# Loads in a line of four, halved first steps, and attention in 64x32 tiles of TensorE, in a fused attention and feed-forward kernel

## The chip, the cores and the metric

The kernel runs on one core of a Trainium2 chip. The metric is the device time of one execution in microseconds (us). A profile of one execution gives, for each engine, when every instruction ran and what it waited for: TensorE (PE, with its weight loads as PEld), VectorE (DVE), ScalarE (ACT), GpSimd (POOL), and SyncE (SP), whose queue issues the DMAs.

## The reference

A linear attention with a quadratic feature map, and a feed-forward block on its result. There are 4 batches, 4 heads, 1088 positions, 32 dimensions per head, r = 8; the block has 4352 tokens of 128 and 2048 hidden units.

```python
def phi(x):
    a = np.einsum('rd,bhsd->bhsr', S1, x)
    b = np.einsum('rd,bhsd->bhsr', S2, x)
    return np.einsum('bhsi,bhsj->bhsij', a, b).reshape(*x.shape[:-1], r * r)
q_p, k_p = (phi(q), phi(k))
kv = np.einsum('bhsf,bhsd->bhfd', k_p, v)
z = np.sum(k_p, axis=2)
num = np.einsum('bhsf,bhfd->bhsd', q_p, kv)
den = np.einsum('bhsf,bhf->bhs', q_p, z)[..., None] + 1e-06
x = num / den                       # heads side by side: 4352 x 128
h = x @ w_in
out = (h * np.clip(h + 3.0, 0.0, 6.0) / 6.0) @ w_out
```

## The kernel before, in words

Tokens lie along the free dimension, in nine chunks: eight of 512 and one of 256 that gathers the ends of all four batches. Each chunk goes through eight steps in the feed-forward block; a step makes 256 hidden units.

*Keys, per batch* (`keys`, `features`): kT is loaded in two groups of 4 and 5 tiles of 128 positions. PE projects them (`abps_k`), ACT copies the result (`ab_k`), POOL or DVE forms the 64 products per head (`ph_k`), PE sums products times v over all positions (`kvps`, 33 columns: 32 of v and one of ones), and ACT copies the sums to `kvb`, in which two heads' blocks stand diagonally.

*Queries of chunks 0 and 1* (`queries`): the same projection and products, then PE transposes the products (`phps`), ACT copies them (`phT`), PE forms numerators and denominators (`nd`, in `divided`), DVE divides (`norm`), PE transposes x (`xt`, into `xps`), and `split` makes of x a rounded part `xh` on ACT and the rest `xl` on DVE or POOL.

*Queries of chunks 2 to 8, called far* (`far_queries`): the projection is two matmuls with 64 weight columns (`mm_far`, tile `abps_q`, L457), DVE transposes in blocks of 32 (`cp_far`, `turn`), and the full transposition goes through DRAM: `wr` writes four pieces (`phd`, L667), `rd` reads them back as `phT` (L672). `nd` then runs in two halves of 256 tokens, each matmul with 32 tokens as weights, all 128 rows and 66 columns (two heads), so that half of the products are with zeros.

*Feed-forward step* (`step`): w_in and w_out come as 64-bit words and are split into a high and a low part by nine DVE and ACT operations per block of 512 (`convert_steps`, tiles `cva_wi`, `cva_wo`). A step takes h = wi_hi xh + wi_lo xh + wi_hi xl (L723, L724, L729), ACT's relu, DVE's gate (`g`), ACT's rounded part (`gh`), POOL's or DVE's rest (`gl`), and three products per 128 units into the output bank `o` (L768, L769, L771).

*Order.* Everything is entered into a list (`Plan`) with a cost per engine, a due time and the buffers it holds. `Plan.order` plays the list through in time and so fixes the order on every engine; the hardware then runs each engine's list in that order. The due times come from constants (`STEP`, `DUES`, `LAG`, `LEADS`, `W_DUE`, `CONV_LEAD`, `LOAD_DUE`). Until 17 us of planned time PE gets filler matmuls (`warm`, L326) where it would be idle. PSUM is three pools: h (2 of two banks), o (2), a (2). In fp32, the profile counts two matmul instructions and two weight loads for each matmul call of the attention. All loads go on SP's queue as soon as the plan has them due and a buffer is free; nothing else holds them back.

Of the kernel before, what the change touches and what calls it, by code (L numbers as in the profile page):

```python
# [15 lines left out]
F32 = mybir.dt.float32  # L16
F32R = mybir.dt.float32r
# [5 lines left out]
P = 128  # L23
HP = P // 2
# [26 lines left out]


# [8 lines left out]
START = {PE: 0.6, ACT: 4.2, DVE: 4.05, POOL: 2.0, SP: 1.18}  # L61
# [3 lines left out]
S_READY = 4.6  # L65
# [9 lines left out]


# [7 lines left out]
STEP = 4.6  # L84
DUES = (154.74, -15.16, 342.66, 122.47)
LAG = 20.51
W_DUE = (-264.43, 162.57, -10.3, 9.86, 223.59, -14.56, -8.54, 128.42)
CONV_LEAD = (-233.02, -43.68, 143.73, 134.72, 228.69, 90.47, 237.81, 136.67, 12.66)
LOAD_DUE = {'kT_0': -98.0, 'wiraw0': -99.0, 'kT_1': -97.0, 'kT_3': -89.0, 'qT_1': -96.0, 'v_3': -95.0, 'v_0': -94.0, 'qT_0': -90.0, 'v_1': -93.0, 'woraw0': -87.0, 'v_2': -88.0, 'kT_2': -92.0, 'wiraw1': -91.0}
LEADS = ({'ab': -122.75, 'cp': -223.0, 'ph': 236.37, 'kv': 270.92, 'kvb': 259.6, 'tr': -22.42, 'trcp': -414.87, 'nd': -219.64, 'norm': 20.99, 'xt': 200.47, 'xh': -420.54, 'xl': 165.56, 'k0': -152.92, 'kld': 94.09, 'vld': 12.64, 'qld': -163.5, 'rd': -4.41, 'xw': 26.17, 'xr': -69.62}, {'ab': 51.61, 'cp': 372.76, 'ph': -99.12, 'kv': 10.45, 'kvb': -57.07, 'tr': -243.35, 'trcp': -85.14, 'nd': 171.45, 'norm': -61.11, 'xt': 74.34, 'xh': 39.91, 'xl': 385.1, 'k0': 34.47, 'kld': 59.11, 'vld': 69.81, 'qld': 111.37, 'rd': 68.22, 'xw': 337.32, 'xr': -5.08}, {'ab': -408.45, 'cp': -279.52, 'ph': 530.56, 'kv': -494.27, 'kvb': 166.7, 'tr': -30.0, 'trcp': -36.58, 'nd': 2.26, 'norm': 255.85, 'xt': -99.65, 'xh': 32.03, 'xl': -230.05, 'k0': 396.51, 'kld': 294.01, 'vld': 22.2, 'qld': 35.72, 'rd': 273.5, 'xw': -349.65, 'xr': 50.89})  # L90


HOLD = 21.82
HOLD_DUE = -27.43
SOON = 22.85
SOON_DUE = 316.94
PATIENCE = 0.75
# [34 lines left out]
class Plan:  # L132
# [56 lines left out]

    def order(self):  # L190
# [9 lines left out]
        while left:  # L200
# [13 lines left out]
            for op in avail:  # L214
                if op.ready > t and len(op.cost) == 1 and all(b.held or any(free[g] for g in b.tags) for b in op.bufs):
                    soon[next(iter(op.cost))].append((op.ready, op.due))
            began = []
            for op in avail:
                if op.ready > t or not all(b.held or any(free[g] for g in b.tags) for b in op.bufs):
                    continue  # L220
# [77 lines left out]
def fused_kernel(ctx: ExitStack, tc: tile.TileContext, qT, kT, v1, sb, w_in, w_out, outT):  # L298
# [73 lines left out]

    def load(tag, shape, name, src, due, dtype=F32, view=None):
        b = Buf((tag,))
        box = []

        def emit(_):
            t = buf(tag, shape, name, dtype)
            box.append(t)
# [5 lines left out]
        return plan.add({SP: ISSUE}, LOAD_DUE.get(name, due), (), emit, [b], moved=n * mybir.dt.size(dtype) / 1e3), b, box  # L385

# [15 lines left out]
    nc.vector.tensor_tensor(s_sb, s_sb, low, op=ALU.add)  # L402
    s_ab = const.tile([P, 2, H, R], F32, name="s_ab")
    nc.scalar.copy(s_ab, s_sb.rearrange("p (h s r) -> p s h r", s=2, r=R))
# [8 lines left out]

    def weights(j, due_i, due_o):
        c = slice(j * WB, (j + 1) * WB)
        for nm, src, view, hi, lo, due, acc in (
            ("wi", w_in[:, c], None, wi_hi, wi_lo, due_i, wi_ops),
            ("wo", w_out_v[:, j * 4 : (j + 1) * 4, :], lambda t: t.rearrange("p (f d) -> p f d", d=P), wo_hi, wo_lo, due_o, wo_ops),
        ):
# [170 lines left out]
    def split(c, due, T, last, xpb, xhb, LEAD):  # L590
# [15 lines left out]
        if xpb.tags == ("xT",):  # L606
            cost = {POOL: 2.35 * n / 1024, **cost}
# [249 lines left out]
```

## Time and profile before

| | |
|---|---|
| three runs | 245.06, 245.56, 245.86 us (median 245.56) |
| the profiled execution | 245.6 us, of which the span from first to last instruction is 243.4 us |
| mean granted TensorE clock | 0.985 |
| busy share of the span: PE, PEld, DVE, ACT, POOL | 97, 75, 75, 67, 58% |
| DMA | 23.82 MB in 18008 packets, mean 98 GB/s |
| first hidden-layer matmul | 24.09 us after the span's start |

A page of the profile gives busy time per engine, the span in 40 slices (a digit is the busy share in tenths; PEclk is the granted clock in tenths of full speed), the DMA queues, the chain of work that ended last, and the costliest groups of instructions. "L557" is a line of the kernel; a count such as x64 is of instructions. Matmuls overlap, so a group's mean duration is longer than the distance from one to the next; the chain's pieces give the latter.

### The profile page before, as it was taken

Reading aid. Unit: us, or ns where it says so; the run is one execution under the profiler, and the core shown is the slowest. Engines: PE = TensorE matmul, PEld = TensorE weight load, DVE = VectorE, ACT = ScalarE, POOL = GpSimd, SP = SyncE. Lnnn points to the kernel's source line nnn. Section 1 sums busy time; section 2 is a strip of 40 time slices with the busy share of each in tenths; the row PEclk is TensorE's granted clock in tenths of the full one; section 3 lists DMA queues with packets and bytes.
Section 4 is the critical chain, followed back from the end, with each engine's and each line's share of the span. In section 5 each row is a group of like instructions: output and inputs, shape, how many; then the busy total and the mean of one; then the engine's idle time right before and its main releaser. Section 6 shows DMA issues by size and latency. Waiting matters only on the chain.

```text
span 243.4 us, 5531 instructions
## 1 busy us (share of the span) xinstructions
PE 234.9 (97%) x2281; PEld 182.4 (75%) x2281; DVE 183.0 (75%) x251; ACT 163.3 (67%) x204; POOL 141.7 (58%) x87
## 2 busy tenths in 40 slices
PE   8949999999999999999999999999999999999994
PEld 2737767676777778877788888888888787888894
DVE  3928999999999689899698875666566676466662
ACT  4425669648859756577399877667777666767771
POOL 2514969976799999249055745444433534944340
PEclk9967999999999999999999999999999999999999
DMA  6996752432033624884443100001000111010010
GB/s 210 383 402 237 256 176 58 151 90 86 3 90 103 168 80 130 212 268 125 137 91 77 46 12 31 0 4 43 0 0 3 43 43 43 3 43 0 0 46 22
DMA packets 18008, 23.82 MB, mean 98 GB/s; under 512 B 1728, under 2 KB 11072, under 8 KB 17984
## 3 DMA queue, kind: packets, MB, share of 16 engines
q1 hardware_dynamic: 17984, 23.48, 30.6%
q8 instruction: 18, 0.29, 0.5%
q14 instruction: 6, 0.05, 0.1%
HBM read 16.26 MB, written 7.21 MB: 96 GB/s over the span
## 4 chain that ended last, share of the span: by engine, by line
PE 91%; issue 2%; DMA 2%; ACT 2%; DVE 1%; SPq 0%
PE h L723 14%; PE h L729 13%; PE o L771 13%; PE o L768 13%; PE h L724 13%; PE o L769 13%; PE nd L557 4%; PE kvps L514 3%; DMA kT<-kT_dram 2%; PE abps_k L452 2%; PE abps_q L457 2%; PE phps L629 1%; PE warm L326 1%; ACT g L736 1%; PE abps_q L452 1%
## 5 line engine op out<-in xcount | busy, mean ns | idle before, releaser
L747 POOL TENSOR_TENSOR gl<-g,gh 128x1024 fp32r<-128x1024 f32 (+1 forms) x45 | 106.4, 2373 | 65.1 <-ACT gh L743 60.4
L739 DVE SCALAR_TENSOR_TENSOR g<-g,h 128x1024 f32<-128x1024 f32 (+1 forms) x72 | 83.0, 1157 | 37.2 <-ACT g L736 36.9
L736 ACT ACTIVATE g<-h 128x1024 f32<-128x1024 f32 (+1 forms) x72 | 70.1, 977 | 35.9 <-PE h L729 35.2
L743 ACT CAST gh<-g 128x1024 fp32r<-128x1024 f32 (+1 forms) x72 | 71.8, 1000 | 14.9 <-DVE g L739 11.8
L723 PE MATMUL h<-xh,wi_hi 128*128 128x512 f32 (+1 forms) x144 | 56.4, 392 | 0.2 <-DVE g L739 0.2
L729 PE MATMUL h<-xl,wi_hi 128*128 128x512 f32 (+1 forms) x144 | 55.4, 386 | 0.0
L724 PE MATMUL h<-xh,wi_lo 128*128 128x512 f32 (+1 forms) x144 | 55.0, 382 | 0.0
L768 PE MATMUL o<-gh,wo_hi 128*128 128x512 f32 (+1 forms) x144 | 55.0, 384 | 0.0
L769 PE MATMUL o<-gh,wo_lo 128*128 128x512 f32 (+1 forms) x144 | 54.5, 381 | 0.0
L771 PE MATMUL o<-gl,wo_hi 128*128 128x512 f32 (+1 forms) x144 | 43.8, 386 | 0.0
L747 DVE TENSOR_TENSOR gl<-g,gh 128x1024 fp32r<-128x1024 f32 (+1 forms) x27 | 31.5, 1171 | 1.7 <-ACT gh L743 1.5
L723 PEld LDWEIGHTS h<-xh,wi_hi 128*128 128x128 f32 x144 | 27.0, 187 | 6.8 <-DVE g L739 0.7
L768 PEld LDWEIGHTS o<-gh,wo_hi 128*128 128x128 f32 x144 | 27.0, 188 | 6.3 <-ACT kvb L539 0.4
L729 PEld LDWEIGHTS h<-xl,wi_hi 128*128 128x128 f32 x144 | 27.0, 187 | 6.0
L769 PEld LDWEIGHTS o<-gh,wo_lo 128*128 128x128 f32 x144 | 27.0, 187 | 5.6
L724 PEld LDWEIGHTS h<-xh,wi_lo 128*128 128x128 f32 x144 | 27.1, 188 | 5.4
L771 PEld LDWEIGHTS o<-gl,wo_hi 128*128 128x128 f32 x144 | 25.9, 187 | 6.2 <-POOL gl L747 0.8
L480 POOL TENSOR_TENSOR ph_k<-ab_k 128x512 f32<-128x512 f32 (+1 forms) x15 | 14.9, 1009 | 15.5 <-ACT ab_k L461 15.5
L480 POOL TENSOR_TENSOR ph_q<-ab_q 128x512 f32<-128x512 f32 x13 | 13.7, 1069 | 3.5 <-DVE ab_q L465 3.5
L557 PEld LDWEIGHTS nd<-kvb,phT 128*32 128x32 f32 (+1 forms) x480 | 9.3, 119 | 3.6 <-issue 3.1
L602 POOL TENSOR_TENSOR xl<-xT,xh 128x512 fp32r<-128x512 f32 x4 | 6.2, 1550 | 9.0 <-ACT xh L598 9.0
L557 PE MATMUL nd<-kvb,phT 128*32 128x66 f32 (+1 forms) x480 | 11.2, 229 | 0.0
(70 smaller groups left out, 165.3 us busy)
## 6 DMA issues: line engine op xcount, KB each, us to landing
phd<-pht SPq DMA_DIRECT2D x24, 128.0 KB, 2.2
phT<-phd SPq DMA_DIRECT2D x6, 512.0 KB, 4.4
wiraw<-w_in_dram SPq DMA_DIRECT2D x4, 512.0 KB, 5.4
qT<-qT_dram SPq DMA_DIRECT2D x8, 256.0 KB, 4.7
woraw<-w_out_dram SPq DMA_DIRECT2D x4, 512.0 KB, 5.9
outT_dram<-os SPq DMA_DIRECT2D x8, 256.0 KB, 2.0
xd<-xt SPq DMA_DIRECT2D x24, 64.0 KB, 1.8
xT<-xd SPq DMA_DIRECT2D x6, 256.0 KB, 2.7
```

The lines of the kernel that those rows point to most:

```text
L480: engines[e].tensor_tensor(out, a_, b_, op=ALU.mult)
L557: nc.tensor.matmul(W["nd"][e : e + w, o : o + 2 * DV], T["phT"][:, p, i : i + w], kvb[batch_of(c0 + i)][:, p, :], start=True, stop=True)
L723: nc.tensor.matmul(T["h"][:, u, :n], wi_hi[:, f], x, start=True, stop=False)
L724: nc.tensor.matmul(T["h"][:, u, :n], wi_lo[:, f], x, start=False, stop=False)
L729: nc.tensor.matmul(T["h"][:, u, :n], wi_hi[:, f], x, start=False, stop=True)
L736: nc.scalar.activation(T["g"][:, :, :n], T["h"][:, :, :n], AF.Relu, bias=3.0, scale=1.0)
L739: nc.vector.scalar_tensor_tensor(T["g"][:, :, :n], T["g"][:, :, :n], 6.0, T["h"][:, :, :n], op0=ALU.min, op1=ALU.mult)
L743: nc.scalar.copy(T["gh"][:, :, :n], T["g"][:, :, :n])
L747: engines[e].tensor_tensor(T["gl"][:, :, :n], T["g"][:, :, :n], T["gh"][:, :, :n].bitcast(F32), op=ALU.subtract)
L768: nc.tensor.matmul(o, wo_hi[:, f], T["gh"][:, u, :n], start=first and u == 0, stop=False)
L769: nc.tensor.matmul(o, wo_lo[:, f], T["gh"][:, u, :n], start=False, stop=False)
L771: nc.tensor.matmul(o, wo_hi[:, f], T["gl"][:, u, :n], start=False, stop=last and u == 1)
```

## The change

1. *Loads.* `FIRST_LOADS` fixes the order of the first 13 loads. From the fifth on, load k has a gate: a POOL copy of one column from the tile of load k - 4 into the tile of load k, which makes it wait for that load's landing and makes load k wait for the copy. All other loads come after the last gate.
2. *Projection weights.* DVE writes `s_ab` (needed first) and ACT copies it to `s_sb`; before, the other way round.
3. *Halves.* For chunk 0 `split` makes `xh` and `xl` in two halves of 256 tokens, each after its own transposition, and its first two steps run their matmuls on each half.
4. *Far projection.* Eight matmuls of 64 rows by 32 weight columns by a quarter of the chunk, for two, into two PSUM banks (one per pair of heads in the upper or lower 64 rows); `cp_far` is two transposes.
5. *Far quotients.* `divided_far` replaces the two halves of `nd`: 64 matmuls of 64 rows by 32 weight columns by 33 columns per 512 tokens, for 32 of 128 rows by 66 columns; the upper 64 rows write one bank, the lower another. `norm` is one operation over both banks.
6. *Write to DRAM.* `wr` issues eight writes per far chunk, for four, half as long each.
7. *Plan.* `room` counts buffers for operations that take two of one pool; all due times and the rules for choosing between engines have new values.

The diff, cut to its core:

```diff
+HALVED = 1
+FIRST = 2
...
-START = {PE: 0.6, ACT: 4.2, DVE: 4.05, POOL: 2.0, SP: 1.18}
+START = {PE: 0.6, ACT: 4.45, DVE: 4.05, POOL: 2.0, SP: 1.18}
...
-S_READY = 4.6
+S_READY = 4.2
...
+AHEAD = 4
+FIRST_LOADS = ("kT_0", "wiraw0", "kT_1", "qT_0", "v_0", "v_1", "qT_1", "woraw0", "kT_2", "wiraw1", "v_2", "woraw1", "qT_2")
...
-STEP = 4.6
-DUES = (154.74, -15.16, 342.66, 122.47)
-LAG = 20.51
+STEP = 6.02
+DUES = (153.97, 226.88, 170.52, 441.39)
+LAG = 31.93
...
+        rank = FIRST_LOADS.index(name) if name in FIRST_LOADS else 0
+        ahead = loads[FIRST_LOADS[rank - AHEAD]] if rank >= AHEAD else None
...
+        def gate(_):
+            old = ahead[2][0].bitcast(U32) if ahead[3] != F32 else ahead[2][0]
+            new = tile().bitcast(F32) if dtype != F32 else tile()
+            nc.gpsimd.tensor_copy(first(new), first(old))
...
+        deps = gates[-1:] if name not in FIRST_LOADS else []
+        if ahead:
+            deps = [plan.add({POOL: 0.12}, due, [ahead[0]], gate, [ahead[1], b])]
+            gates.extend(deps)
...
         def mm_far(_):
-            T["ps"] = bank(pb.tag, f"abps_{name}")
-            for e in (0, HP):
-                nc.tensor.matmul(T["ps"][e : e + HP, : n * HP], s_sb, src[0][:, e * n : (e + HP) * n], start=True, stop=True)
+            T["pss"] = [bank(b.tag, f"abps_{name}_{p}") for p, b in enumerate(pbs)]
+            w = n * Q
+            for p, g in product(range(2), range(4)):
+                r = slice(p * HP, (p + 1) * HP)
+                nc.tensor.matmul(
+                    T["pss"][p][g * Q : (g + 1) * Q, :w],
+                    s_sb[r, p * Q : (p + 1) * Q],
+                    src[0][r, g * w : (g + 1) * w],
+                    start=True,
+                    stop=True,
+                    tile_position=(p * HP, g * Q),
+                )
...
+        def nd(_):
+            W["nd"] = [bank(b.tag, f"nd_{c}_{r}") for r, b in enumerate(nbs)]
+            for t, p, g, r in product(range(nt), range(2), range(4), range(2)):
+                o = (2 * t + p) * DV
+                i = t * P + g * Q
+                f = slice(r * F, (r + 1) * F)
+                nc.tensor.matmul(
+                    W["nd"][r][g * Q : (g + 1) * Q, o : o + DV],
+                    T["phT"][f, p, i : i + Q],
+                    kvb[batch_of(c0 + i)][f, p, r * DV : (r + 1) * DV],
+                    start=True,
+                    stop=True,
+                    tile_position=(r * F, g * Q),
+                )
...
+            for r in range(2):
+                nc.vector.tensor_scalar(den[:, r], nds[r][:, :, D : D + 1], 1e-6, None, op0=ALU.add)
+            nc.vector.reciprocal(rden, den)
...
+            for r in range(2):
+                nc.vector.tensor_tensor(x[:, r], nds[r][:, :, 0:D], rden[:, r].broadcast_to([P, k, D]), op=ALU.mult)
...
+        ranges = [(0, n // 2), (n // 2, n)] if c < HALVED else [(0, n)]
...
-            for e, p in product(range(2), range(2)):
-                k = (2 * e + p) * Q
-                nc.sync.dma_start(d[p, :, :, e * n // 2 : (e + 1) * n // 2].rearrange("f r x -> r f x"), T["turn"][k : k + Q])
+            w = n // 4
+            for g in range(4):
+                src = T["turn"][g * Q : (g + 1) * Q].rearrange("r f (p x) -> r f p x", p=2)
+                for p in range(2):
+                    nc.sync.dma_start(d[p, :, :, g * w : (g + 1) * w].rearrange("f r x -> r f x"), src[:, :, p])
...
+        halved = c < HALVED and fp < FIRST
+        for r, u in product(range(2 if halved else 1), range(2)):
```

More of the change, by code (lines that the diff above doesn't have):

```diff
@@ L100 @@
+HOLD = 9.88
+HOLD_DUE = -2.07
+SOON = 28.52
+SOON_DUE = 75.42
+PATIENCE = 0.61
 @dataclass(eq=False)
@@ L188, in choose, with room @@
         return idle[0]
+    @staticmethod
+    def room(op, free):
+        taken = []
+        for b in op.bufs:
+            if not b.held:
+                g = next((g for g in b.tags if free[g] > taken.count(g)), None)
+                if g is None:
+                    return False
+                taken.append(g)
+        return True
     def order(self):
@@ L214, in order @@
             for op in avail:
-                if op.ready > t and len(op.cost) == 1 and all(b.held or any(free[g] for g in b.tags) for b in op.bufs):
+                if op.ready > t and len(op.cost) == 1 and self.room(op, free):
                     soon[next(iter(op.cost))].append((op.ready, op.due))
@@ L218, in order @@
             for op in avail:
-                if op.ready > t or not all(b.held or any(free[g] for g in b.tags) for b in op.bufs):
+                if op.ready > t or not self.room(op, free):
                     continue
@@ L552, in nd @@
             W["nd"] = bank(nb.tag, f"nd_{c}_{t}")
-            w = HP if c < NEAR else Q
-            for u, p, e in product(range(m), range(2), range(0, P, w)):
+            for u, p, e in product(range(m), range(2), (0, HP)):
                 o = (2 * u + p) * 2 * DV
                 i = (t + u) * P + e
-                nc.tensor.matmul(W["nd"][e : e + w, o : o + 2 * DV], T["phT"][:, p, i : i + w], kvb[batch_of(c0 + i)][:, p, :], start=True, stop=True)
+                nc.tensor.matmul(W["nd"][e : e + HP, o : o + 2 * DV], T["phT"][:, p, i : i + HP], kvb[batch_of(c0 + i)][:, p, :], start=True, stop=True)
         def norm(_):
@@ L674, in far_queries @@
         a = plan.add({DVE: 0.09 + 0.27 * nt}, due - LEAD["tr"], sorted(set(o3), key=o3.index), turn, [phb, turnb])
-        a = plan.add({SP: 4 * ISSUE}, due - LEAD["trcp"], [a], wr, [turnb], moved=n * 1.024)
+        a = plan.add({SP: 8 * ISSUE}, due - LEAD["trcp"], [a], wr, [turnb], moved=n * 1.024)
         rdop = plan.add({SP: ISSUE}, due - LEAD["rd"], [a], rd, [phTb], moved=n * 1.024)
-        norms = []
-        for t in range(0, nt, 2):
-            norms.append(divided(c, due, T, t, min(2, nt - t), rdop, phTb, Buf(ndb), xb, LEAD))
+        norms = [divided_far(c, due, T, rdop, phTb, [Buf(ndb), Buf(ndb)], xb, LEAD)]
         if mixed:
```

154 lines of the change are left out of this document (100 added, 54 removed).

## The prediction

> **What bounds the kernel now.** I read the page first (shares, slices, chain), then the busy table by stage, the chain over the first 24 us, the DMA counts there, and last the chain's far pieces.
>
> ```profile
> span 243.4 us, 5531 instructions
> PE 234.9 (97%) x2281; PEld 182.4 (75%) x2281; DVE 183.0 (75%) x251; ACT 163.3 (67%) x204; POOL 141.7 (58%) x87
> PEclk9967999999999999999999999999999999999999
> PE 91%; issue 2%; DMA 2%; ACT 2%; DVE 1%; SPq 0%
> ```
> TensorE is the bound: 97% busy and 91% of the chain. Only the third and fourth slice show a lower clock. The same by stage (columns: length, then busy and count of PE, PEld, DVE, ACT, POOL; clock; DMA share; GB/s):
> ```profile
> 0.00:12.16 12.16, 10.89 (x222) 6.11 (x222) 7.62 (x18) 5.20 (x12) 4.42 (x13) 1.00 0.84 296
> 12.16:15.57 3.41, 0.00 (x1) 0.00 (x0) 0.48 (x1) 0.08 (x1) 0.00 (x0) 0.80 1.07 390
> 15.57:21.06 5.49, 5.49 (x85) 4.45 (x86) 2.98 (x9) 2.39 (x5) 2.09 (x2) 0.50 0.99 377
> 24.09:240.20 216.11, 215.48 (x1921) 169.82 (x1919) 169.19 (x221) 153.25 (x183) 134.25 (x72) 1.00 0.25 75
> ```
> From the first hidden-layer matmul (24.09) to the last output matmul, PE idles 0.63 of 216.11 us. So time can come only from the first 24 us, or from PE work that gets shorter. The start holds both a dead stretch of 3.41 us, with every engine idle and only DMA at work, and 5.49 us at clock 0.50. The chain there:
> ```profile
> 12.16 3.41 issue
> ...
> 16.05 1.01 PE abps_k L452 x32
> 17.06 1.96 PE nd L557 x32
> ...
> 19.87 0.54 PE warm L326
> ...
> 20.84 0.61 PE warm L326 x2
> ...
> 21.67 0.21 PE warm L326
> ```
> The same work at full clock, and a far projection (columns: start, length, what, count of instructions):
> ```profile
> 28.61 1.24 PE nd L557 x32
> ...
> 53.13 0.58 PE abps_k L452 x32
> 57.64 0.58 PE abps_q L457 x4
> ```
> "Issue" means that PE waited for nothing that the profile shows. I take it for code that hasn't arrived, and argue it from the DMA counts: the whole run's, those of the stall, and what was issued and moved up to 8.3 us.
> ```profile
> q8 instruction: 18, 0.29, 0.5%
> ```
> ```profile
> q1 hardware_dynamic: 1010, 1.31, 104.9%
> q8 instruction: 1, 0.02, 1.7%
> ```
> ```profile
> q1 hardware_dynamic: 1024, 2.11, 74.8%
> issues: line engine op xcount, KB each, median us to landing
> wiraw<-w_in_dram SPq DMA_DIRECT2D x2, 512.0 KB, 5.4
> qT<-qT_dram SPq DMA_DIRECT2D x3, 256.0 KB, 6.9
> v<-v_dram SPq DMA_DIRECT2D x2, 330.0 KB, 5.6
> kT<-kT_dram SPq DMA_DIRECT2D x2, 256.0 KB, 5.1
> woraw<-w_out_dram SPq DMA_DIRECT2D x1, 512.0 KB, 7.4
> kT<-kT_dram SPq DMA_DIRECT2D x1, 320.0 KB, 4.6
> v<-v_dram SPq DMA_DIRECT2D x1, 264.0 KB, 5.6
> sb_raw<-sb_dram SPq DMA_DIRECT2D x1, 64.0 KB, 1.8
> ```
> 18 packets for PE's 4,562 matmuls and weight loads make some 253 instructions a packet. PE stopped after 222 + 222 = 444 of them, a little short of two packets, and the run's first packet moved inside the stall (the counts of 0 to 12.16 us hold none). It would be asked for when one packet was used up, near 8 to 9 us. By 8.3 us the issued loads sum to 4,124 KB (4.22 MB) and 2.11 MB had moved, so 2.11 MB stood in line: 5.4 us at 390 GB/s, which sets a late-comer's turn at 13.7 us, inside the stall. So the packet queued behind the loads.
>
> **The change, part by part.** Sums go against the profiled execution: 243.4 span, 245.6 in all, so 2.2 us lie around the span; the median of the runs is 245.56.
>
> *Loads in line of four.* The first 13 loads keep at most four in flight: a one-column POOL copy waits for the load four places ahead and frees the next. Four neighbours hold at most 512 + 256 + 512 + 264 = 1,544 KB (1.58 MB, 4.0 us of line). The gate and the issue come after the landing, so often only three are moving (about 1.03 MB, 2.6 us). Against 5.4 us the packet comes 1.4 to 2.8 us sooner, and the stall falls from 3.41 to between 0.6 and 2.0; I take 1.4, a gain of 2.0. With a short stall the clock should hold for the most part. At 0.50 nd took 1.96 and abps_k 1.01, at full clock 1.24 and 0.58: 1.15 lost there, some 0.25 more in the projection beside them; I take 1.0 of the 1.4 back. The gates stand on POOL ahead of the key products, behind loads that land by 5 to 8 us; if one lands late, POOL's product and then kv wait for it, and the loads behind wait in SP: bounded by the gain itself, since line and stall are the same bytes. The projection weights made one DVE step earlier save an ACT copy that waits for kT_0 anyway: nothing.
>
> *Halved first steps.* Chunk 0's two norms come one after the other; splitting x lets the first hidden matmul follow the first. It can only replace the filler ("warm" 0.54 + 0.61 + 0.21 = 1.36); I take 0.8. The columns streamed are the same. The start in all: 2.0 + 1.0 + 0.8 = 3.8 (bounds 0 and 3.41 + 1.4 + 1.36 = 6.2).
>
> *Far quotients and projections in 64x32 tiles.* Far nd, the matmul after it, and kv, whose shape is near:
> ```profile
> 60.97 1.06 PE nd L557 x64
> 62.03 0.43 PE h L729
> ...
> 68.95 0.70 PE kvps L514 x60
> ...
> 88.23 0.60 PE nd L557 x32
> ```
> Far nd stands in the chain four times as x64 and five as x32: 4 x 1.06 + 5 x 0.60 = 7.24 us. After, each of six and a half chunks has 64 matmuls of two instructions, 128 for 64, with 33 columns for 66 on eight tiles for four. No row here has two row bands at work. If the bands overlap wholly, an instruction costs a quarter of 1.06/64 = 16.6 ns, 4.1 ns, 0.53 a chunk; if not at all, it costs what kv's 33-column one does, 0.70/60 = 11.7 ns, 1.50 a chunk. Both ends are equally near in shape (kv has the columns, nd the operands), so I take the middle, 1.0: 6.5 us, 0.7 less (bounds: 3.8 less, 2.5 more). One nd for two saves two re-entries; the matmul after one takes 0.43 for 0.23: 0.4.
> Weighed against this, the Trainium skill's "TensorEngine Tiling (Array Packing)", section Instruction Overhead, says that a matmul costs some 60 cycles however few its columns, and not to tile a dimension that is already small. By it 33 columns cost nearly what 66 do, nd would be 128 x 8.3 ns = 1.06 a chunk, and the sum would lose the 0.7; kv's 11.7 ns at half of nd's columns leans that way.
> The projection: 0.58 for 4 instructions of 256 columns on two tiles becomes 16 of 128 columns on eight. Fully overlapped 0.29, without the bands 0.58; nearer the overlap, since halved weights already run side by side in kv and nd: 0.40, six and a half times 0.18 = 1.2 less (bounds 1.9 and 0). PE work in all: 0.7 + 0.4 + 1.2 = 2.3 less.
>
> *Around the tiles.* Two banks are now held at once by projection and by quotient, of the two that "a" has; the x64 pieces already used both. On DVE two transposes stand for one, and one reciprocal goes:
> ```profile
> L465 DVE STREAM_TRANSPOSE ab_q<-abps_q x7: 318/450/451, 22.6 to 191.4; 128x256 f32<-128x256 f32 x6, 128x128 f32<-128x128 f32 x1
> L566 DVE RECIPROCAL rden<-den 128x8 f32<-128x8 f32 x17 | 3.5, 203 | 0.6
> ```
> 2 x 0.318 - 0.450 = +0.19, less 0.20: nothing. If DVE were late, the next far chunk's projection would wait for both banks; DVE is busy 169 of the 216 us. SP issues eight writes for four per far chunk:
> ```profile
> 50.45 1.80 SPq L667 DMA_DIRECT2D phd<-pht  x4
> ```
> ```profile
> 54.45 0.38 SPq L672 DMA_DIRECT2D phT<-phd  x1
> ```
> ```profile
> phT<-phd SPq DMA_DIRECT2D x6, 512.0 KB, 4.4
> ```
> That is 1.8 us more before phT is read back, and later loads queue behind it. Chunk 2's read lands at 54.45 + 4.4 = 58.9, its nd starts at 60.97: the cover is 2.1 us, so 1.8 is hidden, barely. Without cover, PE would stand up to 1.8 for the first far chunk; later ones can be started earlier. *The new due times* reorder all engines; from 24.09 on PE has 0.63 us to win and everything to lose, so I count nothing.
>
> Sum: 3.8 + 2.3 = 6.1 off the span: 237.3, and 239.5 in all.
>
> **Rivals.**
> *A. The code doesn't come sooner.* The line is shorter, but the stall and the cold clock stay. For it: DMA is saturated (share 1.07) with four in flight too, and the link from line to stall is inferred. Against: line and delay agree (13.7 against a packet inside the stall). Then only the 2.3 and 0.5 of the halves come: 240.6 span, 242.8. The Trainium skill's "DMA: Bandwidth & Descriptors", section Queues, rings and completion order, says that each DMA engine takes turns between queues after every packet; by that rule a code packet wouldn't wait for the whole line, which would be this rival, and the trace's agreement with a full line speaks against it.
>
> *B. The row bands don't run together.* Nothing in the trace shows that they do. Then nd is 2.5 dearer, the projection unchanged: 243.4 - 3.8 + 2.5 - 0.4 = 241.7 span, 243.9.
>
> *C. Slower: code runs out in the quotients.* A far nd is now 128 matmuls and 128 weight loads, 256 instructions: a whole packet in about 1 us, where half of one went before. If each of the seven bursts ends in a wait for the next packet (in the stall's counts 1.7% of 16 engines over 3.41 us, 0.93 us of transfer alone), PE idles seven times. It decides from (6.1 + 0.7)/7 = 1.0 us a burst; at 1.3 the span is 243.4 - 6.1 + 9.1 = 246.4, 248.6 in all. For it: the stall at 12.16 is this very thing. Against:
> ```profile
> 25.00:30.00 5.00, 5.00 (x217) 3.73 (x216) 4.72 (x10) 2.75 (x6) 5.00 (x7) 1.00 0.74 255
> ```
> 433 instructions went through in 5 us with PE never idle and DMA at 0.74; and a burst stands between hidden-layer steps, which use only 45 instructions in 5 us, so the next packet has time.
>
> **How the numbers follow.** My forecast (start and tiles both pay, 236 to 242) has 0.60, A 0.14, B 0.14, C 0.12. The time is that of the forecast, 239.5. Its own range goes from 236.0 (start 6.2, tiles 3.4) to 242.0 (start 1.9, tiles 1.7). The range takes in A and B and leaves out C and the extremes: 235.8 to 244.6. About 0.3% (0.74 us) is what a measurement of this kernel can tell from no change. Faster by more (below 244.8): the forecast, A and B but for the cases where a poor start and unpaired bands meet, 0.81. Within it: 0.07. Slower: C, 0.12.
>
> **What would show it.** The chain's issue piece after 12 us: about 1.4 or shorter, and the first code packet before 13 us. The granted clock: at most one stretch at 0.50 before 25 us. The first hidden matmul by 20.3 us (24.09 - 3.8) or sooner. Far nd: one x128 piece near 1.0 us a chunk; the far projection, x16, near 0.40. From there to the end PE idle under 1.5 us. The prediction is wrong if the stall is still over 3 us (A), if nd takes 1.4 (B), if issue pieces of 1 us follow the nd pieces (C), or if PE now waits in the first 60 us for DVE's weight conversions or, in nd, for phT: none of these is in the sum.

## The result: slower by 3%, and the profile after

The changed kernel took 253.40 us (median of 4 runs, 251.84 to 255.22) beside 245.47 for the kernel before: a ratio of 1.033 (1.026 to 1.039). Run again later with the experiments it gave 252.01 (6 runs), ratio 1.025 (1.021 to 1.029). The forecast was 239.5, with 235.8 to 244.6. Ratios here compare undisturbed executions only, so one can lie a little off the quotient of the two medians; a point is one per cent of the kernel before. The profiled execution took 252.8, with a span of 251.0 against 243.4.

The page of the changed kernel (span, busy row, granted clock, PE's code queue, shares of the chain):
```profile
span 251.0 us, 6639 instructions
PE 235.6 (94%) x2788; PEld 184.7 (74%) x2788; DVE 191.5 (76%) x261; ACT 162.6 (65%) x205; POOL 129.1 (51%) x90
PEclk9999779999999999999999999999999999999999
q8 instruction: 22, 0.36, 0.6%
PE 81%; DMA 8%; DVE 4%; issue 3%; SPq 2%; ACT 0%; DVEq 0%
```
PE's busy time rose by 0.7 us (234.9 to 235.6), and its idle time from 8.5 to 15.4 us: nine tenths of the loss is waiting. PE has 2 x 507 instructions more and needs 22 code packets for 18. Where it waits, by stage (columns as in the table before):
```profile
0.00:12.13 12.13, 10.56 (x221) 6.04 (x222) 6.73 (x16) 5.11 (x11) 6.13 (x21) 1.00 0.75 246
...
13.65:33.04 19.39, 13.24 (x434) 10.18 (x433) 15.52 (x34) 6.92 (x16) 7.53 (x8) 0.91 0.92 322
33.04:60.00 26.96, 25.92 (x301) 19.83 (x298) 22.62 (x33) 20.98 (x29) 24.04 (x18) 0.94 0.18 55
60.00:125.00 65.00, 62.83 (x1067) 48.16 (x1066) 52.49 (x80) 41.21 (x47) 55.93 (x28) 1.00 0.44 128
```
The first hidden-layer matmul starts at 33.04 instead of 24.09. Up to it PE idles 9.24 us (33.04 less the 10.56 and 13.24 busy), where it was 4.69 of 24.09; from 33 to 60 it idles 1.04, and from 60 to 125 another 2.17. The chain in the start, and then, from the timeline (start, length, engine, line, operation, tiles), the last pieces of chunk 0's x, which the first hidden step needs:
```profile
12.13 1.52 issue
...
24.55 1.71 issue
...
27.52 1.42 PE kvps L595 x80
28.94 0.94 PE abps_k L521 x34
29.88 2.42 issue
...
33.10 0.51 PE h L850
```
```profile
19.00 0.37 ACT L720 CAST xh<-xps 128x256 fp32r<-128x256 f32 x1
19.40 0.76 DVE L724 TENSOR_TENSOR xl<-xps,xh 128x256 fp32r<-128x256 f32 x2
```
Chunk 0's x is whole at 20.16 (19.40 + 0.76), and DVE finishes the low part of the first block of w_in at 14.48. Yet the hidden layer waits 13 us more, because in the new order PE must first issue key projections (abps_k), key-value sums (kvps) and transposes of other chunks. These are short instructions in great number. Up to the first hidden matmul PE stops three times for "issue", 5.65 us in all, two of them (4.13) after x is whole; in the start before it stopped once, for 3.41. Beside these stand waits for data. PE's table of waits (in all, how often, the longest):
```profile
PE abps_k L521 <- issue: 4.1, 2, 2.4
PE h L850 <- DVE g L867: 1.9, 2, 1.0
PE abps_k L521 <- DMA kT<-kT_dram: 1.5, 2, 0.9
PE abps_q L521 <- issue: 1.5, 1, 1.5
PE nd L666 <- issue: 1.3, 1, 1.3
PE abps_k L521 <- DVE x L648: 1.0, 1, 1.0
```
Issue comes to 6.9 us, where the whole run before had 3.4 + 0.4; data waits (for DVE and for keys) to 4.4, where it had 0.6 (for DVE and ACT). So there are two candidates of about the same size, code and data.

### The profile page after: what moved, and what is told of

It is laid out like the page before. It is cut to its first block, busy times and chain, and to the rows that moved or that the text cites. A ratio compares the mean times of both kernels' runs of the same rounds, so it can differ in the third digit from the quotient of the medians.

```text
span 251.0 us, 6639 instructions
## 1 busy us (share of the span) xinstructions
PE 235.6 (94%) x2788; PEld 184.7 (74%) x2788; DVE 191.5 (76%) x261; ACT 162.6 (65%) x205; POOL 129.1 (51%) x90
## 4 chain that ended last, share of the span: by engine, by line
PE 81%; DMA 8%; DVE 4%; issue 3%; SPq 2%; ACT 0%; DVEq 0%
PE h L850 13%; PE o L896 12%; PE o L899 12%; PE o L897 12%; PE h L856 12%; PE h L851 12%; DMA kT<-kT_dram 5%; PE nd L666 3%; PE kvps L595 3%; PE abps_k L521 2%; DMA xT<-xd 2%; DMA phT<-phd 2%; DVE xl L724 1%; SPq L817 1%; DVE g L867 1%
## 5 line engine op out<-in xcount | busy, mean ns | idle before, releaser
L875 POOL TENSOR_TENSOR gl<-g,gh 128x1024 fp32r<-128x1024 f32 x38 | 91.7, 2427 | 82.9 <-ACT gh L871 62.5
L875 DVE TENSOR_TENSOR gl<-g,gh 128x1024 fp32r<-128x1024 f32 (+1 forms) x34 | 37.7, 1110 | 1.0 <-ACT gh L871 1.0
L850 PEld LDWEIGHTS h<-xh,wi_hi 128*128 128x128 f32 x148 | 28.3, 191 | 9.8 <-DVE g L867 3.5
L856 PEld LDWEIGHTS h<-xl,wi_hi 128*128 128x128 f32 x148 | 28.3, 191 | 5.8 <-issue 0.2
L851 PEld LDWEIGHTS h<-xh,wi_lo 128*128 128x128 f32 x148 | 28.4, 192 | 5.2
L561 POOL TENSOR_TENSOR ph_k<-ab_k 128x512 f32<-128x512 f32 (+1 forms) x17 | 16.5, 992 | 14.5 <-ACT ab_k L540 10.8
L561 POOL TENSOR_TENSOR ph_q<-ab_q 128x512 f32<-128x512 f32 x14 | 16.2, 1174 | 1.7 <-DVE ab_q L546 1.1
L521 PE MATMUL abps_k<-s_ab,kT 128*32 128x64 f32 (+1 forms) x252 | 6.8, 234 | 6.7 <-issue 4.1
L521 PEld LDWEIGHTS abps_k<-s_ab,kT 128*32 128x32 f32 (+1 forms) x252 | 5.2, 121 | 9.0 <-issue 5.7
L540 ACT COPY ab_k<-abps_k 128x256 f32<-128x256 f32 (+1 forms) x8 | 3.2, 399 | 13.3 <-PE abps_k L521 11.9
```

Source lines behind the costliest of these rows:

```text
L521: nc.tensor.matmul(out[e : e + w], src[0][:, t * P + e : t * P + e + w], s_ab.rearrange("p s h r -> p s (h r)"), start=True, stop=True)
L561: engines[e].tensor_tensor(out, a_, b_, op=ALU.mult)
L850: nc.tensor.matmul(T["h"][:, u, i:j_], wi_hi[:, f], x, start=True, stop=False)
L851: nc.tensor.matmul(T["h"][:, u, i:j_], wi_lo[:, f], x, start=False, stop=False)
L856: nc.tensor.matmul(T["h"][:, u, i:j_], wi_hi[:, f], x, start=False, stop=True)
L875: engines[e].tensor_tensor(T["gl"][:, :, :n], T["g"][:, :, :n], T["gh"][:, :, :n].bitcast(F32), op=ALU.subtract)
```

## The experiments

Theory **CODE** (called ORDER in the first expectations, since it lays the shortage to the new order): the loss is code that comes too late. The new order puts the instruction-dense work in one stretch, the far tiles add instructions, and packets of code arrive more slowly than such work uses them up. Rivals: **LINE** (held-back loads make keys and weights late), **TILES** (the tile forms cost PE time, or their eight writes make phT late), and **ORDER BY ITSELF** (the order brings waits for data, and the stalls only fill them). "In its own order" below means that the planner's costs, buffers and constants stay, so every engine issues its operations in the same sequence and only what an operation issues differs.

**1. The line alone, on the order before.** Edit, in the load's emission of the kernel before:
```diff
+            if 4 <= len(line) < 13:
+                old, kind = line[-4]
+                nc.gpsimd.tensor_copy(first(t.bitcast(F32) if dtype != F32 else t), first(old.bitcast(U32) if kind != F32 else old))
+            line.append((t, dtype))
             nc.sync.dma_start(view(t) if view else t, src)
```


> The kernel before with its own order and constants; the first 13 loads alone stand in a line of four (a POOL copy from the load four ahead into the new tile, as the change does it). Theory ORDER (the loss comes from the new order, which puts 13 us of short instructions ahead of the first hidden step, so that PE's code runs out there): the line by itself does not cost: first code packet near 11.5 us instead of 13.21, the 3.41 us stall at 12.2 falls to 1.5, time 242 to 245.5. Theory LINE (holding loads back makes keys and weights late): keys and weights come 2 us or more later, first hidden matmul after 25 us, time 247 to 250. Theory TILES: nothing of the loss is in this run, 242 to 246.

Measured: 249.92 us, ratio 1.016 (1.010 to 1.022). LINE's numbers are met, in the time and in the first hidden matmul (27.17 us). Of CODE's, the length of the stall nearly is (1.71 for 1.5), but the time isn't, and the stall (at 19.33) and the first packet (18.74) come seven microseconds later than it said.
```profile
PE kvps L523 <- POOL ph_k L489: 5.3, 1, 5.3
PE phps L638 <- issue: 1.7, 1, 1.7
PE kvps L523 <- issue: 1.0, 1, 1.0
```
These rows are PE's waits. The long stall falls from 3.41 to 1.71 (not because the packet came sooner after PE's need: see the table under "Loads in line" below), and the time is lost in one new wait: POOL, stuck in the gate copies behind loads, brings the key product late, and PE waits 5.3 us for it. So a line costs when its gates stand ahead of work that PE needs soon. The changed kernel's table of waits has no such row, so the 5.3 belongs to this placement of the gates.

**2. The line opened, in the changed kernel's own order.** The POOL copies stay and read a ready tile:
```diff
-            old = ahead[2][0].bitcast(U32) if ahead[3] != F32 else ahead[2][0]
...
-            nc.gpsimd.tensor_copy(first(new), first(old))
+            nc.gpsimd.tensor_copy(first(new), ident[:, :1])
```


> The changed kernel in its own order, with the line opened: the POOL copies stay where they are, but read a tile that is ready, so that all of the first loads are in flight as SP issues them. Theory ORDER: the code packets now wait behind more loads, the stall at 12.1 us grows from 1.52 to about 3.4 and the two at 24.6 and 29.9 stay over 1 us each: 252 to 256. Theory LINE: keys come early, the 1.55 us of waits for key loads go, and so does most of the start's loss of 4.6 us: 246 to 250. Theory TILES: no change, 252 to 254.

Measured: 251.03, ratio 1.021 (1.015 to 1.026), not told apart from the changed kernel's 1.025, and in none of the three ranges. The first stall, which CODE expected to grow to 3.4, came out at 1.69 for 1.52: a miss. The 1.5 us of waits for kT shrink to 0.8, and issue stalls take their place (9.1 us over the run).

But the edit opens the line only in part. Most of the copies stand behind POOL's first key product in POOL's order, and the loads wait for the copies there. The fifth load leaves SP 1.84 us earlier (3.05 for 4.89), most later ones about half a microsecond. The seventh, in the changed kernel and here:
```profile
7.96 0.33 SPq L414 DMA_DIRECT2D qT<-qT_dram  x1
```
```profile
7.42 0.33 SPq L414 DMA_DIRECT2D qT<-qT_dram  x1
```
So LINE falls as far as it means that a load waits for the landing of another. What all the first loads at once would do in this order, to keys or to packets of code, no run shows.

**3. Code asked for earlier.** Each warm-up matmul as four of a quarter of the columns:
```diff
-        nc.tensor.matmul(warm, ones[:, :P], ones, start=True, stop=True)
+        w = CH // 4
+        for i in range(4):
+            nc.tensor.matmul(warm[:, i * w : (i + 1) * w], ones[:, :P], ones[:, :w], start=True, stop=True)
```


> The changed kernel in its own order, each warm-up matmul of 512 columns issued as four of 128 columns: the same columns, three more matmuls and weight loads each (some 130 instructions more), early, while the DMA line is empty. Theory ORDER (code late): PE gets to the point where it asks for the first packet before the loads fill the line; the first packet lands before 9 us and the stall of 1.52 at 12.1 goes; the later packets are asked for earlier too, and of the stalls at 24.6 and 29.9 (4.13 us together) half or more goes: 248.5 to 251. Theories LINE and TILES: no change or the price of more instructions, 252 to 254.

Measured: 251.37, ratio 1.027 (1.020 to 1.034): a miss. The stall did not go, it came earlier and grew (3.23 us at 10.15). But it tells what sets its place. The stage from 0 to the first long stall in this run, and in the run with the line opened:
```profile
0.00:10.15 10.15, 8.26 (x221) 7.52 (x222) 4.93 (x13) 4.17 (x9) 4.75 (x18) 1.00 0.74 236
```
```profile
0.00:11.71 11.71, 9.90 (x221) 5.97 (x222) 6.67 (x16) 5.10 (x11) 6.16 (x23) 1.00 0.79 260
```
PE stops after 221 matmuls and 222 weight loads, at 10.15 us here, at 11.71 there, at 12.13 in the changed kernel, and after 222 and 222 at 12.16 in the kernel before; with the line alone it was 222 and 222 at 19.33. Five runs, nine microseconds apart, one count, at three different instructions (a transpose, a query projection, a key-value sum). Waits for data would not agree on a count. What this edit spent early on fillers, PE lacked two microseconds later.

**4. Fewer instructions, in both kernels' own orders.** Key projections of all batches in 64 rows instead of 32 for batches 1 to 3, key-value sums in 64 rows instead of 32 (the trace shows each of these fp32 matmuls as two, each with its weight load, so the records fall by twice the expected counts, from 2,788 to 2,392):
```diff
-                for e in range(0, P, w):
+                for e in range(0, P, HP):
...
-            for h, f in product(range(H), range(0, F, Q)):
+            for h, f in product(range(H), range(0, F, F)):
...
-                    K["ps"][e : e + Q, w],
-                    T["ph"][:rows, t, h * F + f : h * F + f + Q],
+                    K["ps"][e : e + F, w],
+                    T["ph"][:rows, t, h * F + f : h * F + f + F],
```


> The changed kernel in its own order; the near short work is issued in fewer instructions: every key tile's projection as 2 matmuls of 64 rows (batches 1 to 3 had 4 of 32) and every tile of the key-value sums as 4 matmuls of 64 rows (it had 8 of 32): about 200 matmuls, 400 instructions with their weight loads, fewer of some 5,580, and most of them in the first 60 us. Theory CODE (PE's code cannot come as fast as the short instructions use it up): the stalls of 1.5, 1.7 and 2.4 us at the start shrink to under 2.5 us together, first hidden matmul 2 to 4 us earlier than in the changed kernel: 248 to 251. Rival ORDER-BY-ITSELF (the start is long because of data waits that the order brings, and the stalls only fill them): waits for loads and for DVE take the stalls' place, 252 to 254. Rival WIDTH (64-row tiles cost PE more than they save): PE busy goes up by 1 us or more.

> The kernel before in its own order, with the same two forms of fewer instructions. Theory CODE: the stall of 3.41 us at 12.2 comes later and is shorter by 1 to 3 us: 242 to 244.5. Rival WIDTH: PE busy up by 1 us or more and the time with it, 245.5 to 248. If the stall is not one of code at all, it stays at 3.4 and the time within 0.5 us of 245.2.

Measured: the changed kernel 246.92, ratio 1.002 (0.998 to 1.006); the kernel before 242.08, ratio 0.984 (0.980 to 0.988). Code is what both kernels are short of. The changed kernel's page, and the stage that ends just behind the start of its first hidden matmul:
```profile
PE 235.0 (97%) x2392; PEld 185.8 (76%) x2392; DVE 191.3 (79%) x261; ACT 162.7 (67%) x205; POOL 129.0 (53%) x90
```
```profile
0.00:26.83 26.83, 23.59 (x415) 17.12 (x415) 20.00 (x46) 12.73 (x30) 13.77 (x31) 1.00 0.90 316
```
Its table of waits has no issue row left (the longest row is h's for DVE's g, 1.5 us), the granted clock is 1.00 over the whole run, and the first hidden matmul comes at 26.76, 6.3 us sooner. By then PE has issued 414 matmuls, in the changed kernel 655 (221 + 434). The kernel before with the same edit, page and stage:
```profile
PE 234.7 (98%) x1885; PEld 184.0 (77%) x1885; DVE 183.0 (76%) x251; ACT 163.1 (68%) x204; POOL 141.9 (59%) x87
```
```profile
0.00:20.08 20.08, 17.68 (x256) 11.63 (x257) 13.50 (x31) 9.62 (x21) 7.45 (x16) 1.00 0.92 331
```
Its 3.41 us stall is gone, the clock is 1.00 throughout this stage, and the first hidden matmul comes at 19.83 for 24.09. This is the gain that the line of four was to bring, had without touching a load. WIDTH has a part as well: at full clock five key tiles of sums take 1.02 us in 32 rows and 1.43 in 64 (timeline; the first row is the kernel before, the second the same with fewer instructions):
```profile
73.62 1.02 PE L514 MATMUL kvps<-v,ph_k 128*32 128x33 f32 x80
```
```profile
70.22 1.43 PE L514 MATMUL kvps<-v,ph_k 128*64 128x33 f32 x40
```
The form of the sums that is dearer for PE wins all the same, where code is short.

The two runs bound CODE, too. The same edit brings the kernel before 1.6 points and the changed kernel 2.3 to 3.1 (from 1.025 or 1.033 to 1.002). Only the difference, 0.7 to 1.5 points, is loss that the change made by its code; 1.8 points, 1.002 against 0.984, remain between the kernels when neither of them stops for code. So CODE alone falls, and the rest has to be found.

**5. Order and halves alone**, the gates on a ready tile and both tile forms undone (experiments 2 and 6 together); the same with fewer instructions; and then without the halves (x copied whole, whole first steps).

> The changed kernel's constants, order and first steps by halves alone: the line is opened (the POOL copies read a ready tile) and both far tile forms are undone. Theory CODE AND ORDER: what is left of the loss is the start's: first hidden matmul at 29 to 32 us, code stalls of 5 us or more together before it, 248 to 250. If the line were a loss of its own beside it, 246 to 247.5; if the tiles were all of the loss, 244 to 246.

> The run of order and halves alone, with the two forms of fewer instructions as well. Theory CODE: most of that run's stalls go, 2 to 4 us below it: 245 to 247.5. Rival ORDER-BY-ITSELF: within 1 us of it.

> The run of order and halves alone with fewer instructions (ratio 1.001), with the halves undone too: chunk 0's x copied whole and its first two steps in whole 512-column matmuls, at the places of the second half. What is left of the change is its order. ORDER BY ITSELF: x is whole 6 us before the first hidden matmul, so the halves neither help nor hurt: ratio 0.998 to 1.004. If the halves were the loss of 1.7 points, 0.984 to 0.988.

> The changed kernel with fewer instructions (ratio 1.002), line and tiles in, with the halves undone in the same way. ORDER BY ITSELF: 0.998 to 1.006. If the halves cost: 0.985 to 0.990.

Measured: 249.84, ratio 1.015 (1.009 to 1.020); 246.38, ratio 1.001 (0.997 to 1.006); without halves 246.68, ratio 1.001 (0.998 to 1.004); and the changed kernel with fewer instructions and without halves 246.99, ratio 1.004 (1.000 to 1.008). The halves do nothing that can be measured. The order alone, against the old one, costs 1.5 points with the instructions as they were and 1.7 with fewer (1.001 against 0.984): it is a price of its own, the same whether or not code is short, and ORDER BY ITSELF holds for it. To the order belong here the loads' order with its copies and the choices between DVE and POOL (with fewer instructions DVE is busy 191.8 us for 183.0 in the old order, POOL 128.5 for 141.9); no run takes these apart. PE's waits in the run without tiles or halves, gates on a ready tile, with fewer instructions:
```profile
PE h L831 <- DVE g L850: 1.8, 2, 1.0
PE abps_k L519 <- issue: 1.1, 1, 1.1
PE abps_k L519 <- DVE wi_lo L387: 0.8, 1, 0.8
PE kvps L581 <- DMA v<-v_dram: 0.6, 1, 0.6
```
PE's idle time is 8.7 us here (span 243.5 less 234.8 busy), 5.7 with the old order (240.4 - 234.7). Of the 3.0 us between them, 1.3 lie ahead of the first hidden matmul (3.70 for 2.40), 0.9 from there to 60 us and 0.8 up to 125. The row named issue is hardly code: the key projection that waits there starts 0.10 us after DVE's last x of chunk 1 (22.55), which reads the quotient's bank. In the changed kernel the same wait goes by DVE's x (23.92, then 24.02), and in the run with halves by nd:
```profile
22.65 0.69 PE L519 MATMUL abps_k<-s_ab,kT 128*64 128x64 f32 x16 [1.08 <-issue]
```
```profile
21.53 0.69 PE L519 MATMUL abps_k<-s_ab,kT 128*64 128x64 f32 x16 [1.01 <-PE nd L623]
```
In some executions the clock falls as well. The profiled execution of the changed kernel with fewer instructions and without halves was such a one, with a span of 247.0; three of its stages, and two rows of PE's waits:
```profile
20.50:24.00 3.50, 2.06 (x53) 1.65 (x48) 3.15 (x9) 1.24 (x4) 2.29 (x3) 1.00 1.04 406
24.00:27.30 3.30, 2.31 (x46) 2.21 (x48) 3.30 (x6) 0.40 (x3) 1.90 (x2) 0.74 1.04 412
27.30:30.70 3.40, 3.40 (x47) 3.14 (x44) 1.99 (x4) 1.20 (x3) 1.73 (x2) 0.50 0.94 292
```
```profile
PE kvps L595 <- POOL ph_k L561: 1.4, 1, 1.4
PE abps_k L521 <- DVE x L648: 1.0, 1, 1.0
```
PE is busy for 2.06 of 3.50 and 2.31 of 3.30 us, waiting for DVE's x and POOL's key product, and then runs at 0.50 with nothing to wait for; its busy time is 237.6 for 235.0. So the order's price is some 3 us of waits for data and banks, and a cold clock on top in some executions. That the waits bring the clock down is read from these rows, not shown: the changed kernel with fewer instructions waits 1.0 us for the same bank and keeps 1.00.

**6. The tiles undone: both, and one at a time.** Far quotients as 128-row, 66-column matmuls again, far projection as two 64-row matmuls, one transpose and four writes again.

> The changed kernel in its own order (the planner's costs and buffers are left as they are), with both far tile forms undone in what is issued: the far projection in 2 x 64-row form into one bank with one transpose and four writes to DRAM, the far quotient as 32 matmuls of 66 columns over 128 rows into two banks. Theory TILES: PE busy falls by 0.7 us or more, the code stall of 1.28 us at 119 and the 0.82 us wait at 107 go: 249.5 to 251. Theory ORDER: the start is as in the changed kernel (first hidden matmul near 33 us, stalls at 12.1, 24.6, 29.9), at most 1.5 us come back: 251.5 to 253.5. Theory LINE: the same as ORDER.

> The changed kernel in its own order with the far quotients alone put back to 32 matmuls of 66 columns over 128 rows a chunk, in two banks (416 matmuls, 832 instructions fewer of 5,580 in all). Theory CODE: the tiles' share of the loss (some 4 us by the run with both tile forms undone) is that of their instructions, and most of these are the quotients': 249.5 to 251.5. Rival WRITES (the eight writes that the far projection's new layout needs make phT and xT late): 252.5 to 254, and the gain is in the next run.

> The changed kernel in its own order with the far projection alone put back (2 x 64 rows into one bank, one transpose, four writes to DRAM instead of eight). Theory CODE: some 56 instructions fewer, PE 0.2 us a chunk more: 253 to 255. Rival WRITES: 249.5 to 251.5, and the 0.82 us wait at 107 us goes.

Measured: 249.43, ratio 1.016 (1.012 to 1.020), with both undone (TILES' 249.5 to 251 is all but met, the 251.5 to 253.5 of the two others missed; the 1.28 us stall in nd is gone); 248.45, ratio 1.011 (1.006 to 1.015), without the quotient tiles; 249.87, ratio 1.019 (1.016 to 1.023), without the projection tiles. Against the 1.025 of the changed kernel (another session) the tiles are worth about 0.9 points. The parts don't add up (both undone gains no more than one). Stalls also differ where nothing before them was changed: the first one, ahead of all far tiles, took 1.19, 2.49 and 1.32 us in the three profiles. CODE's numbers are missed in both single runs, which came out lower. WRITES' are met in the projection's run and missed in the quotient's; so neither is borne out.

**7. The shortage taken away, with and without the tiles.** 64-row sums for batches 0 and 1 alone, in the changed kernel and with both tile forms undone, beside the changed kernel itself.

> The changed kernel as it is, beside the runs below. Expected 251 to 255, with a spread of some 3 us from how many code packets come late; if it comes out at 251 or below, the runs with parts undone show smaller effects than they seemed to.

> The changed kernel in its own order, with 64-row key projections throughout and 64-row key-value sums for batches 0 and 1. Theory CODE: no long stall before 40 us, PE 1.6 us less than with 64 rows throughout (246.9 there): 244 to 247, and at 1.0 of the clock 243.5. Theory TILES-BY-THEIR-CODE: a stall of about 1 us returns near 67 or 119 us, where the 256 instructions of a quotient piece follow other short work.

> The same with both far tile forms undone. If the tiles cost by their code alone, and the code now comes in time, 0 to 1 us from the run with the tiles: 243.5 to 246.5. If they cost by PE time or by late phT, 2 us or more below it. What is left against the kernel before with the same forms (241.2) is the order's own: waits of h for DVE's g near 51 us, of the key projection for the quotient's bank, some 2 to 4 us.

Measured: 252.01; 250.15, ratio 1.021 (1.016 to 1.026); 246.03, ratio 1.004 (1.001 to 1.008). The second is a miss: with 32-row sums in batches 2 and 3 most of the loss was back. The first rows of its waits:
```profile
PE kvps L596 <- DMA v<-v_dram: 2.1, 2, 1.9
PE nd L667 <- issue: 1.5, 1, 1.5
PE h L857 <- DVE x L687: 1.4, 1, 1.4
```
Stalls in nd and kvps are there again, beside a late load and a late x; how much each is worth this run can't tell. With the tiles the kernel is 1.6% slower here; with 64 rows throughout the same pair, from experiments 4 and 5, stands at 1.002 and 1.001. So a cost of the tiles shows where PE is held up, in part by late code, and none that can be measured shows where it isn't.

**8. All quotient tiles in one row band.**
```diff
-                f = slice(r * F, (r + 1) * F)
+                f = slice(0, F)
...
-                    tile_position=(r * F, g * Q),
+                    tile_position=(0, g * Q),
```


> The changed kernel with all 64 quotient tiles of a chunk in the upper row band (what is left out: the lower 64 rows' products, so the heads of the second column are not computed). If the two bands run beside each other, a chunk's quotient takes clearly longer than the 1.21 to 1.29 us of the changed kernel, 1.7 us or more; if the tiles are bound by how fast PE takes instructions, it stays at 1.2 to 1.3 us, and the bands bring nothing at this size.

Measured: one execution, 256.43 us, of a kernel that leaves out the products of the lower 64 rows. A chunk's quotient in the timeline, first in the changed kernel (and the piece that a stall cuts), then in one band:
```profile
74.32 1.29 PE L666 MATMUL nd<-kvb,phT 64*32 64x33 f32 x128
...
117.89 1.27 PE L666 MATMUL nd<-kvb,phT 64*32 64x33 f32 x127
120.45 0.19 PE L666 MATMUL nd<-kvb,phT 64*32 64x33 f32 x1 [1.28 <-issue]
```
```profile
73.81 1.47 PE L666 MATMUL nd<-kvb,phT 64*32 64x33 f32 x128
```
Neither expectation: the bands overlap, but by 0.18 of 1.47 us. Two bands cost 10.1 ns a matmul, one band 11.5.

**9. A version that beats both.** The kernel before with 64-row projections, and 64-row sums for batches 0 and 1, or for batch 0 alone.
```diff
+            m = F if b < 2 else Q
-            for h, f in product(range(H), range(0, F, Q)):
+            for h, f in product(range(H), range(0, F, m)):
```


> The kernel before in its own order, key projections in 64-row matmuls, key-value sums in 64-row matmuls for batches 0 and 1 alone (up to 33 us), batches 2 and 3 as before in 32-row matmuls, which take 0.19 us a key tile of PE for 0.28. Theory CODE: nothing runs out before 33 us, later the hidden steps (8 instructions in a microsecond) give the code time to come: PE 18 x 0.09 = 1.6 us less than with 64 rows throughout, 240 to 241.5. Rival: code runs out at the 32-row sums of batches 2 and 3, 242 to 243.5.

> The same with 64-row key-value sums for batch 0 alone. Theory CODE: another 9 x 0.09 = 0.8 us of PE less, but 72 instructions more between 21 and 30 us, where packets still stand in line behind loads: 239.5 to 242.5; a stall near 25 to 30 us would tell that the code is short there too.

Measured: 241.20, ratio 0.984 (0.981 to 0.986), and 242.49, ratio 0.988 (0.986 to 0.991). The page with two batches:
```profile
PE 233.0 (98%) x2027; PEld 182.2 (76%) x2029; DVE 182.8 (76%) x251; ACT 163.0 (68%) x204; POOL 141.8 (59%) x87
```
With two batches PE's busy time falls by 1.7 (234.7 to 233.0; expected 1.6) and the profiled span by 1.4 (240.4 to 239.0); by the ratios it isn't told apart from 64 rows throughout. With batch 0 alone a stall of 0.99 us stands at 22.71, as CODE feared: that is where the trade turns. Between these two runs only the sums of batch 1 differ, and the form that is dearer for PE gains 0.4 points.

## Why the prediction was wrong

**The step that failed** is "the new due times reorder all engines; from 24.09 on PE has 0.63 us to win and everything to lose, so I count nothing". The order alone costs 1.5 to 1.7 points, 3.7 to 4.2 us, about half of the loss. In the changed kernel most of the new idle time lies in the start (4.55 of 6.9 us), where the prediction counted gains only: the first hidden matmul moved from 24.09 to 33.04, behind 655 matmuls for 364. Where code is not short, the order's waits are spread over the first 125 us (experiment 5). The prediction's marks for late data, waits for DVE's weight conversions or, in nd, for phT, don't stand in the profile's table; PE waited in the first 60 us for DVE's x (1.01) and g (1.04), which neither the sum nor a mark named.

**Code: the diagnosis right, the count missing.** That the stall at 12.16 us is code holds (experiments 3 and 4); that the code came late because of the loads ahead of it isn't shown (next paragraph). The prediction applied it to that one stall and, as rival C, to the quotients. It never counted the instructions that the new order and tiles ask for in the whole start. That is the other 0.7 to 1.5 points.

**Loads in line: the stall's size met, its reason not shown.** Forecast: stall 1.4 and first packet before 13 us. Measured: 1.52, and the packet at 11.46. In the prediction the packet comes sooner because it stands behind fewer loads. When it is asked for no view shows; as a mark take PE's 220th matmul or weight load, about half of the 444. (The prediction has the asking near 8 to 9 us, after one packet of 253; by 9.00 PE had issued 141, and 254 only by 9.86.) From stage rows and the DMA counts of short windows, in us:

| run | 220th | PE stops | packet starts to move | PE goes on | from 220th to packet |
|---|---|---|---|---|---|
| before | 9.72 | 12.16 | 13.21 | 15.57 | 3.49 |
| line alone (1) | 15.45 | 19.33 | 18.74 | 21.04 | 3.29 |
| changed | 9.31 | 12.13 | 11.46 | 13.65 | 2.15 |
| changed, once more (7) | 8.88 | 12.28 | 11.53 | 13.79 | 2.65 |
| gates on a ready tile (2) | 8.91 | 11.71 | 11.08 | 13.40 | 2.17 |
| fillers in four (3) | 8.78 | 10.15 | 10.28 | 13.37 | 1.50 |
| before, fewer instructions (4) | 12.02 | no stop | 14.12 | | 2.10 |

With the line alone the packet came hardly sooner after the mark (3.29 for 3.49); its stall is shorter because PE spent the rest of its supply more slowly (3.88 us for 2.44). And without any line, with fewer instructions, it came after 2.10. So the forecast stall was met (rival A's, that it stays, is refuted), but whether by the line, by the new order or by chance this record doesn't tell: count the hit as luck. The gain (3.41 to 1.52) was given back twofold, as PE stopped twice more for 4.13. The 1.0 us of cold clock did not come: two slices stand at 0.7, later than before. The named risk, POOL held by the gates, is real (5.3 us in experiment 1), though no such wait stands in this kernel's table. What the line costs or pays in the new order stays open (1.016 with it, 1.015 with the gates on a ready tile, both with the tiles undone, but that edit hardly moves the loads).

**Halved steps, 0.8: nothing.** x was whole at 20.16, the first hidden matmul at 33.04; without the halves the time is the same (experiment 5).

**Tiles: 2.3 less forecast, 0.4 more measured.** With fewer instructions and the clock at 1.00 throughout, PE is busy 235.0 us with the tiles (experiment 4) and 234.6 without (experiment 5). The far quotients take 1.1 more, where 0.7 less was forecast (with tiles, then without); the far projections take 3.0 for 4.4, 1.4 less for a forecast 1.2:
```profile
L666 PE MATMUL nd<-kvb,phT 64*32 64x33 f32 x832 | 8.6, 201 | 0.4 <-DMA phT<-phd 0.4
```
```profile
L651 PE MATMUL nd<-kvb,phT 128*32 128x66 f32 x416 | 7.5, 222 | 0.0
```
The chain of the changed kernel has both pieces:
```profile
110.87 0.38 PE abps_q L529 x16
...
114.22 1.22 PE nd L666 x77
```
The projection was right (forecast 0.40, before 0.58). The quotient was not: 1.22 in the chain, for 1.06 before and a forecast 1.0 (the row names 77 instructions of the piece; the timeline has all 128, in 1.29). The mid-point between full overlap and none was the wrong choice; 10.1 ns lies next to the unpaired bound of 11.7 that kv's row gave. For the quotient, rival B holds nearly in full, though 1.4 was its mark; for the projection it doesn't. The Trainium skill's "TensorEngine Tiling (Array Packing)", section Instruction Overhead, warns against tiling a dimension that is already small. The trace agrees: twice the matmuls at half the columns cost more, and the prediction's estimate by that page, 1.06, was nearer than the 1.0 that it took (at 1.06 a chunk, 6.9 us in all, 0.35 of the 0.7 would have been left, not nothing).

**Rival C, at 0.12, had the mechanism and the wrong place.** It set code against the quotients' bursts, and one of these does end in a stall (1.28 at 119.17). The others don't; that the hidden steps before them give the code time, as its counter-argument said, fits but was not tested. It should have been asked of the whole start: there no hidden steps stand between.

**Eight writes, "hidden, barely".** With the projection and its writes undone the ratio is 1.019 for 1.025, in another session; that the writes alone cost anything isn't shown. In the changed kernel's second profile nd does wait 0.7 us for phT, but so it does with four writes in the last run of experiment 9 (0.6).

## What to carry to other kernels

Count instructions as a resource of its own, stage by stage, beside busy time: where an engine runs short instructions while loads fill DMA, a form with half the instructions can win although it is dearer for the engine (here 0.29 us a key tile of sums against 0.20, and the kernel with both shorter forms 1.6% faster). When "issue" stands in the chain, compare the count of instructions up to the stall between two runs: the same count at another time means code, not data. New constants for an order are a change of their own: cost them by what stands ahead of the first work that matters, and by which data it needs by then, before counting anything else.

## What the runs showed of the hardware

- PE stopped after the same 443 or 444 matmuls and weight loads in five runs, at 10.15 to 19.33 us. That fits a first supply of somewhat over 444 instructions (others are not counted in the rows). Later packets bring about 256 each, an estimate from differences between runs: 1,014 matmuls and loads more go with 4 packets more (changed kernel and before), 792 fewer with 3 fewer (changed kernel, experiment 4). The prediction's 253 divides all 4,562 by the 18 packets, though the first 444 came ahead of them. The Trainium skill's "Runtime: NRT & Kernel Launch", section Instruction fetch mechanics, has such blocks of 256 instructions, 2,048 instructions held for TensorE, and a crossing into the next block that is mostly hidden. The size of the blocks agrees; the first stop at 444, with stalls of 3.41, 1.52, 1.71 and 2.42 us, agrees neither with 2,048 nor with "mostly hidden".
- From the start of the first packet to PE going on, 2.19 to 2.36 us passed in the runs of the table where the packet itself took 0.94 to 0.98 us, and 3.09 where it took 1.75. When a packet is asked for, and how long it then stands behind loads, was not measured.
- Two row bands at work on 33 columns brought 12% (1.47 to 1.29 us for 128 matmuls), not a factor of two.
